# Fused attention, Fourier mixing and two feed-forward stages: tables split on the host, g_norm moved to the head outputs, the start reordered

## The chip, the cores and the metric

The kernel runs on one core of a Trainium2 chip. The metric is device microseconds of one execution. Three runs of the kernel before took 1918.46 to 1920.63 us, median 1919.91.

## The reference

Three layers, all in float32, with batch 8, 8 heads, sequence 576, head size 64, model width 512:

```python
kv  = einsum('bhsd,bhse->bhde', k, v)
out = einsum('bhsd,bhde->bhse', q, kv)
x   = out / sqrt(mean(out*out, -1) + 1e-06) * g_norm     # per head, then heads side by side
u   = x + real(fft(fft(x, axis=1), axis=2))              # sequence, then width
un  = (u - mean(u)) / sqrt(var(u) + 1e-06)
x2  = u + relu(un @ w_ch1) @ w_ch2                       # 512 -> 2048 -> 512
u2  = x2 + (x2.T @ U @ V).T                              # rank 32 over the sequence
y   = u2 + relu(u2 @ w1b) @ w2b
```

The weights of both feed-forward stages arrive as 64-bit floats (seen by the kernel as pairs of 32-bit words) and are made 32-bit on the chip.

## The kernel before

**Precision by splitting.** Most matmuls use operands of type fp32r, a rounded float32. A number is held as a high part (a copy on ACT, which rounds) and a low part (the number less the high part, on DVE or POOL). A product is three matmuls: low by high, high by low, high by high. Names end in `h` and `l`.

**The main loop** has 18 blocks of 512 tokens, 9 for the first feed-forward stage (phase A) and 9 for the second (phase B), with 16 steps each. Step `n` loads one 128-wide strip of the hidden layer: `split_w2` and `split_w1` (two steps ahead) split the weights, `emit_l1` runs 12 matmuls into `h`, ACT makes `gh` (line 174) and DVE `gl` (line 175), and `emit_l2` of the step before runs 12 matmuls that need `gl`. Then the step's side tasks follow. On each engine instructions run in the order in which this code issues them; a step's `gl` on DVE therefore stands behind all that the side tasks of the step before put on DVE.

**Side tasks.** While block `j` of phase A runs, `batch_tasks(j + 1)` prepares the next batch: `t_o` (q times kv into PSUM; ACT squares it, line 265, and copies it out, line 266; DVE sums the squares, line 268; POOL raises to the power -1/2, line 270), `t_norm` (DVE multiplies by that, line 281; POOL multiplies by `g_norm`, line 283), `t_fold_s`/`t_fold_e` (sums and differences of mirrored tokens and columns, lines 296, 297 and 302), `t_fold_h`/`t_fold_l` (their high and low parts; `pile` for the last tokens), `t_s1` (Fourier along the sequence), `t_s2` (along the width, and the update of `x`). In block 0 the side tasks also hold 13 steps of `w_conv`, the conversion of a pair of weight tiles: a load into one of two `raw` buffers, two ACT and three DVE instructions per tile, and a POOL addition (line 98). The load of the next pair waits for the conversion of this one.

**The start** does batch 0 in line, before the loop: kv, q, the five tiles of `t_o`, `t_norm` (all of it on DVE and ACT here), folds, `t_s1`, `t_s2`, then the row statistics (`t_ln`: `bn_stats`, line 472), four transposes (`t_tr`) and the first `emit_l1`. `load_tables` fetches six tables of cosines and sines, `split_table` splits them on ACT and POOL. Three weight pairs are converted in between. All loads and stores are issued by SP, in order.

Of the kernel before, what the change touches and what calls it, by code (L numbers as in the profile page):

```python
# [34 lines left out]

HMIN, HMAX = (float(v) for v in np.array([0x38000000, 0x47EFFFFF], np.uint32).view(np.float32))
# [3 lines left out]
def kernel(ctx: ExitStack, tc: tile.TileContext, qT, kvm, gn, w1a, w2a, w1b, w2b,  # L40
# [5 lines left out]
    wpool = ctx.enter_context(tc.tile_pool(name="wpool", bufs=NF))  # L46
# [5 lines left out]
    ps_s = ctx.enter_context(tc.tile_pool(name="ps_s", bufs=2, space=PSUM))  # L52

# [21 lines left out]
    def raw_load(src, n):  # L75

        r = com.tile([128, 512, 2], U32, tag="raw", name="raw", bufs=2)
        nc.sync.dma_start(out=r[:, 0:n].rearrange("p n w -> p (n w)"), in_=src.bitcast(U32))
        return r[:, 0:n]

    def conv_a(raw, out):
# [5 lines left out]
        pw = com.tile([128, 512], U32, tag="cv1", name="cv1", bufs=2)[:, 0:n]  # L87
# [110 lines left out]
    pa = ctx.enter_context(tc.tile_pool(name="pa", bufs=1))  # L198
# [40 lines left out]
    def t_kv(b, half):  # L239
# [10 lines left out]
        nc.vector.tensor_copy(out=kvbd[64:128, pairs, 64:128], in_=pv[64:128, :, 64:128])  # L250
# [3 lines left out]
    def t_o(b, k):  # L254
# [11 lines left out]
        nc.scalar.activation(out=s["x"][:m, g, c, :], in_=ps[:m, :], func=AF.Copy)  # L266
# [5 lines left out]
    def t_norm(b, k):  # L272
# [4 lines left out]
        if b == 0 and g == 1:  # L277
# [4 lines left out]
        eng = nc.vector if b == 0 else nc.gpsimd  # L282
        eng.tensor_tensor(out=xv, in0=xv, in1=gnb[:m].unsqueeze(1).to_broadcast([m, H, D]), op=ALU.mult)
# [3 lines left out]
    def t_fold_s(b, c):  # L287
        s = st[b]
        if c == 0:
# [6 lines left out]
        nc.vector.tensor_tensor(out=f[:m, 0, c, 0:DM], in0=x[:m, 0, c], in1=x[:m, 1, c], op=ALU.add)  # L296
        nc.gpsimd.tensor_tensor(out=f[:m, 1, c, 0:DM], in0=x[:m, 0, c], in1=x[:m, 1, c], op=ALU.subtract)
# [110 lines left out]
    def batch_tasks(b):  # L408
# [3 lines left out]
        for c in range(3):  # L412
# [3 lines left out]
            t[c + d + 3] += [lambda c=c: t_fold_s(b, c), lambda c=c: t_fold_e(b, c, 0), lambda c=c: t_fold_h(b, c, 0)]  # L416
# [30 lines left out]

    def t_ln_load(j):
        un[j] = [pa.tile([128, DM], F32, tag="un", name=f"un{j}_{t}", bufs=4) for t in range(4)]
        for t in range(4):  # L450
            load_u(un[j][t], 4 * j + t)

    def t_ln_first(cc):

        x = st[0]["x"]
        if cc == 0:
            un[0] = [pa.tile([128, DM], F32, tag="un", name=f"un0_{t}", bufs=4) for t in range(4)]
# [9 lines left out]
    def t_ln(j, ts=range(4)):  # L467
        if 0 in ts:
            lns[j] = [pa.tile([128, 4, w], F32, tag=f"ln{w}", name=f"ln{j}_{w}") for w in (6, 2, 1)]
# [69 lines left out]
    def x_new(j):  # L539
        pool = pa if j % 2 else pbx["pb"]  # L540
        return tuple(pool.tile([128, 4, BT], F32R, tag=t, name=f"{t}b{j}") for t in ("xh", "xl"))

    def t_b_tables(step):
# [68 lines left out]
    def t_u2(j, dc):  # L612
        pb = pbx["pb"]
        blk = NB + j
        if dc == 0 and j:
# [53 lines left out]
    CONV = (1, 1, 0, 1, 13)  # L669
# [10 lines left out]
    with tc.manual_schedule():  # L680
# [7 lines left out]
        nc.sync.dma_start(out=gnb, in_=gn)  # L688
        w_load(0)
        w_load(1)  # L690
        load_tables()
# [202 lines left out]
```

## Time and profile before

| | |
|---|---|
| profiled execution | 1920.98 us, span 1919.2 us |
| median of three runs | 1919.91 us |
| busy | PE 1816.7, DVE 966.8, ACT 773.9, POOL 751.5 us |
| start, until the first `h` matmul | 75.25 us |
| block 0, until the first `h` matmul of step 16 | 150.05 us |
| blocks 1 to 6 | 111.9 or 113.4 us each |

PE is the matmul engine (PEld its weight loads), DVE the vector engine, ACT the scalar engine, POOL GpSimd, SP the queue of transfers. Times are microseconds from the span's start. PEclk is the granted clock of the matmul engine as a share of full speed. A wait is put down to what came last.

### The profile page before, as it was taken

Reading aid. Unit: us, or ns where it says so; the run is one execution under the profiler, and the core shown is the slowest. Engines: PE = TensorE matmul, PEld = TensorE weight load, DVE = VectorE, ACT = ScalarE, POOL = GpSimd, SP = SyncE. Lnnn points to the kernel's source line nnn. Section 1 sums busy time; section 2 is a strip of 40 time slices with the busy share of each in tenths; the row PEclk is TensorE's granted clock in tenths of the full one; section 3 lists DMA queues with packets and bytes.
Section 4 is the critical chain, followed back from the end, with each engine's and each line's share of the span. In section 5 each row is a group of like instructions: output and inputs, shape, how many; then the busy total and the mean of one; then the engine's idle time right before and its main releaser. Section 6 shows DMA issues by size and latency. Waiting matters only on the chain.

```text
span 1919.2 us, 22748 instructions
## 1 busy us (share of the span) xinstructions
PE 1816.7 (95%) x8520; PEld 1504.9 (78%) x8520; DVE 966.8 (50%) x1458; ACT 773.9 (40%) x1462; POOL 751.5 (39%) x592
## 2 busy tenths in 40 slices
PE   3767999999999999999999999999999999999999
PEld 3646878788787878878888888888888888888887
DVE  5887875757757575755443333333333233333222
ACT  4445543444444344433434343334333343333332
POOL 4576554555445555533322223222222222222322
PEclk7889999999999999999999999999999999999999
DMA  4524424142242414202223201010101010100000
GB/s 148 208 101 168 170 90 146 56 165 106 109 135 86 158 56 160 89 12 81 72 99 109 84 0 50 1 44 1 50 1 44 1 50 1 45 1 22 1 23 23
DMA packets 61760, 142.14 MB, mean 74 GB/s; under 512 B 11129, under 2 KB 13898, under 8 KB 58834
## 3 DMA queue, kind: packets, MB, share of 16 engines
q1 hardware_dynamic: 61650, 140.69, 20.9%
q8 instruction: 67, 1.10, 0.2%
q14 instruction: 43, 0.35, 0.1%
HBM read 102.88 MB, written 36.73 MB: 73 GB/s over the span
## 4 chain that ended last, share of the span: by engine, by line
PE 81%; DVE 9%; POOL 4%; ACT 3%; issue 2%; DMA 1%; SPq 0%; DVEq 0%; POOLq 0%; ACTq 0%
PE h L169 12%; PE h L171 12%; PE h L170 12%; PE acc L195 7%; PE acc L194 7%; PE acc L193 7%; PE acc L189 5%; PE acc L191 5%; PE acc L190 5%; DVE f L302 2%; PE kv L245 2%; DVE eh L331 1%; POOL ss L270 1%; PE o L263 1%; PE pt L603 1%
## 5 line engine op out<-in xcount | busy, mean ns | idle before, releaser
L147 POOL TENSOR_TENSOR w1l<-w,w1h 128x512 fp32r<-128x512 f32 x274 | 355.5, 1297 | 971.7 <-ACT w1h L146 948.4
L175 DVE SCALAR_TENSOR_TENSOR gl<-h,gh 128x512 fp32r<-128x512 f32 x288 | 198.3, 689 | 389.7 <-ACT gh L174 389.5
L174 ACT ACTIVATE gh<-h 128x512 fp32r<-128x512 f32 x288 | 171.5, 596 | 500.5 <-PE h L171 500.4
L155 DVE TENSOR_TENSOR w2l<-w,w2h 128x512 fp32r<-128x512 f32 x283 | 231.8, 819 | 188.6 <-ACT w2h L154 187.8
L189 PE MATMUL acc<-w2h,gl 128*128 128x512 f32 x576 | 233.8, 406 | 41.2 <-DVE gl L175 41.1
L154 ACT ACTIVATE w2h<-w 128x512 fp32r<-128x512 f32 x288 | 181.2, 629 | 159.5 <-PE acc L195 112.0
L190 PE MATMUL acc<-w2l,gh 128*128 128x512 f32 x576 | 230.0, 399 | 10.0 <-POOL w2l L155 10.0
L169 PE MATMUL h<-xl,w1h 128*128 128x512 f32 x576 | 228.6, 397 | 1.4 <-DVE xl L493 1.4
L169 PE MATMUL h<-xlb,w1h 128*128 128x512 f32 x576 | 229.8, 399 | 0.0
L191 PE MATMUL acc<-w2h,gh 128*128 128x512 f32 x576 | 229.4, 398 | 0.0
L171 PE MATMUL h<-xhb,w1l 128*128 128x512 f32 x576 | 226.8, 394 | 0.0
L170 PE MATMUL h<-xhb,w1h 128*128 128x512 f32 x576 | 226.6, 393 | 0.0
L171 PE MATMUL h<-xh,w1l 128*128 128x512 f32 x576 | 225.4, 391 | 0.8 <-POOL w1l L147 0.8
L195 PE MATMUL acc<-gh,w2h 128*128 128x512 f32 x576 | 225.0, 391 | 0.0
L170 PE MATMUL h<-xh,w1h 128*128 128x512 f32 x576 | 224.8, 390 | 0.0
L194 PE MATMUL acc<-gl,w2h 128*128 128x512 f32 x576 | 224.7, 390 | 0.0
L193 PE MATMUL acc<-gh,w2l 128*128 128x512 f32 x576 | 224.4, 390 | 0.0
L146 ACT ACTIVATE w1h<-w 128x512 fp32r<-128x512 f32 x288 | 179.9, 625 | 35.5 <-POOL w L98 35.5
L189 PEld LDWEIGHTS acc<-w2h,gl 128*128 128x128 f32 x576 | 111.1, 193 | 74.5 <-DVE gl L175 51.4
L190 PEld LDWEIGHTS acc<-w2l,gh 128*128 128x128 f32 x576 | 111.5, 194 | 33.5 <-POOL w2l L155 11.4
L191 PEld LDWEIGHTS acc<-w2h,gh 128*128 128x128 f32 x576 | 111.2, 193 | 24.0
L169 PEld LDWEIGHTS h<-xlb,w1h 128*128 128x128 f32 x576 | 108.3, 188 | 25.5 <-issue 2.6
(162 smaller groups left out, 2731.8 us busy)
## 6 DMA issues: line engine op xcount, KB each, us to landing
kv<-in_kvm SPq DMA_DIRECT2D x14, 1280.0 KB, 8.3
q<-in_qT SPq DMA_DIRECT2D x8, 1220.0 KB, 7.5
x_d<-x2o SPq DMA_DIRECT2D x36, 256.0 KB, 2.1
x2f<-x_d SPq DMA_DIRECT2D x36, 256.0 KB, 4.0
outT<-o SPq DMA_DIRECT2D x36, 256.0 KB, 2.0
raw<-in_w1a SPq DMA_DIRECT2D x16, 512.0 KB, 10.1
raw<-in_w2a SPq DMA_DIRECT2D x16, 512.0 KB, 4.2
u_d<-x SPq DMA_DIRECT2D x32, 256.0 KB, 2.5
```

The costliest lines, as they stand in the source:

```text
L147: (nc.vector if n in on_dve else nc.gpsimd).tensor_tensor(out=al, in0=a, in1=f32(ah), op=ALU.subtract)
L155: (nc.gpsimd if n in CLP else nc.vector).tensor_tensor(out=cl, in0=c, in1=f32(ch), op=ALU.subtract)
L169: nc.tensor.matmul(out=h, lhsT=ah[:, kc, :], rhs=xl[:, kc, :], start=(kc == 0), stop=False)
L170: nc.tensor.matmul(out=h, lhsT=ah[:, kc, :], rhs=xh[:, kc, :], start=False, stop=False)
L171: nc.tensor.matmul(out=h, lhsT=al[:, kc, :], rhs=xh[:, kc, :], start=False, stop=(kc == 3))
L175: nc.vector.scalar_tensor_tensor(out=gl, in0=h, scalar=0.0, in1=f32(gh), op0=ALU.max, op1=ALU.subtract)
L189: nc.tensor.matmul(out=a, lhsT=gl[:, tt], rhs=ch, start=s, stop=False)
L190: nc.tensor.matmul(out=a, lhsT=gh[:, tt], rhs=cl, start=False, stop=False)
L191: nc.tensor.matmul(out=a, lhsT=gh[:, tt], rhs=ch, start=False, stop=e)
L193: nc.tensor.matmul(out=a, lhsT=cl[:, tt], rhs=gh, start=s, stop=False)
L194: nc.tensor.matmul(out=a, lhsT=ch[:, tt], rhs=gl, start=False, stop=False)
L195: nc.tensor.matmul(out=a, lhsT=ch[:, tt], rhs=gh, start=False, stop=e)
```

## The change

- The tables are split on the host. They arrive as three tensors, are copied by DMA to a DRAM tile and from there to SBUF; `split_table` is gone.
- `t_o`: DVE multiplies the PSUM tile by `g_norm` into `x`, in place of ACT's copy. `t_norm` has no second multiplication left. The squares are still taken of the unscaled tile.
- `t_norm` of batch 1 has the tiles of `g == 1` on ACT (eight scalings each), as batch 0 has. Both `kvbd` copies of batch 1 are on ACT.
- The difference folds of batch 0 are on DVE, with those of later batches still on POOL.
- In the start: the second Fourier stage takes slices 2, 0, 1; the first weight conversions come after `t_s1` and between the slices; row statistics are taken in two parts; the second weight pair is converted after `t_ln`, and `split_w1(0)` comes earlier.
- `un` and `res` are single tiles of four; in phase B the even blocks use their buffers; pools are opened in another order.

```diff
-    def load_tables(): ...
-    def split_table(nm): ...
+    def load_tables(step, t={}):
+        for k, src in enumerate(tabs):
+            if step == 0:
+                t[k] = dram.tile(list(src.shape), F32, tag=f"tab_d{k}", name=f"tab_d{k}")
+                nc.sync.dma_start(out=t[k], in_=src)
+                continue
+            s = at.tile(list(src.shape), F32R, name=f"tab{k}")
+            nc.sync.dma_start(out=f32(s), in_=t[k])
...
 def t_kv
-        nc.vector.tensor_copy(out=kvbd[64:128, pairs, 64:128], in_=pv[64:128, :, 64:128])
+        if b == 1:
+            nc.scalar.activation(out=kvbd[64:128, pairs, 64:128], in_=pv[64:128, :, 64:128], func=AF.Copy)
+        else:
+            nc.vector.tensor_copy(out=kvbd[64:128, pairs, 64:128], in_=pv[64:128, :, 64:128])
...
 def t_o
-        nc.scalar.activation(out=s["x"][:m, g, c, :], in_=ps[:m, :], func=AF.Copy)
+        nc.vector.tensor_tensor(out=heads(s["x"][:m, g, c]), in0=heads(ps[:m, :]),
+                                in1=gnb[:m].unsqueeze(1).to_broadcast([m, H, D]), op=ALU.mult)
...
 def t_norm
-        if b == 0 and g == 1:
+        if b < 2 and g == 1:
...
-        eng = nc.vector if b == 0 else nc.gpsimd
-        eng.tensor_tensor(out=xv, in0=xv, in1=gnb[:m].unsqueeze(1).to_broadcast([m, H, D]), op=ALU.mult)
...
 def t_fold_s
+        eng = nc.gpsimd if b and p else nc.vector
+        eng.tensor_tensor(out=f[:m, p, c, 0:DM], in0=x[:m, 0, c], in1=x[:m, 1, c], op=(ALU.add, ALU.subtract)[p])
...
 def x_new
-        pool = pa if j % 2 else pbx["pb"]
+        tags = ("xh", "xl") if j % 2 else ("un", "res")
+        pools = (pa, pa if j else pbx["pb"])
...
 the start
+        load_tables(0)
         w_load(0)
         w_load(1)
-        load_tables()
+        load_tables(1)
...
+        for p in range(2):
+            for e in range(2):
+                t_s1(0, p, e)
+        conv_b(*conv_a(raws.pop(0), w_new(0)))
+        t_s2(0, 2)
+        t_ln_first(2)
         t_s2(0, 0)
         t_ln_first(0)
+        split_w1(0)
+        t_s2(0, 1)
+        t_ln_first(1)
+        t_ln_stats(0, (0, 2))
+        conv_b(*conv_a(raws.pop(1), w_new(1)))
         w_next((0, 1))
+        t_ln_stats(0, (1, 3))
         load_q(1)
-        conv(CONV[1])
-        split_w1(0)
         t_kv(1, 0)
         t_kv(1, 1)
...
         t_ln(0)
-        conv(CONV[2])
+        conv(1)
         for t in range(4):
             t_tr(0, t)
```

Three places show what moves. The first is DVE in the start, from the end of `t_o` to the first folds of batch 0 (`x` is the batch's tile, `f` the folded one); before:

```order
L268 TENSOR_REDUCE ss_199<-sq_198 98x8 [waits Activation_49]
L269 TENSOR_SCALAR ss_199<-ss_199 98x8 [waits DVE_49]
L281 TENSOR_TENSOR x_197<-x_197,ss_199 128x512 [waits Pool_49]
L283 TENSOR_TENSOR x_197<-x_197,gnb 128x512 [waits DMAHW5_49,DVE_49]
L283 TENSOR_TENSOR x_197<-x_197,gnb 128x512 [waits Activation_49]
L296 TENSOR_TENSOR f_261<-x_197 128x512 [waits DMAHW2_49,DMAHW1_49,DMAHW3_49,DMAHW0_49,DVE_49]
L302 TENSOR_TENSOR f_261<-f_261 128x256 [waits DVE_49]
```

And in the change:

```order
L266 TENSOR_TENSOR x_208<-o_4_251,gnb 98x512 [waits Activation_49]
L269 TENSOR_REDUCE ss_210<-sq_209 98x8
L270 TENSOR_SCALAR ss_210<-ss_210 98x8 [waits DVE_49]
L282 TENSOR_TENSOR x_208<-x_208,ss_210 128x512 [waits Pool_49]
L296 TENSOR_TENSOR f_270<-x_208 128x512 [waits DMAHW1_49,DMAHW2_49,DMAHW0_49,DMAHW3_49,DVE_49]
L301 TENSOR_TENSOR f_270<-f_270 128x256 [waits DVE_49]
```

The multiplication by `gnb` has moved ahead of the sums, one for each of five tiles, and now it is the one that waits for ACT's square; the two behind the scaling are gone.

The second is DVE between the second Fourier stage and the first transposes (`cv` and `w` are weight conversions, `ln` the row statistics); before:

```order
L385 TENSOR_TENSOR x_197<-x_197,de_2_469 34x255 [waits DVE_49]
L89 TENSOR_SCALAR cv_482<-cv_482 128x512 [waits Activation_49]
L91 TENSOR_SCALAR w_0_1_480<-cv_482 128x512 [waits DVE_49]
L89 TENSOR_SCALAR cv_487<-cv_487 128x512 [waits Activation_49]
L91 TENSOR_SCALAR w_0_1_481<-cv_487 128x512 [waits DVE_49]
L96 SCALAR_TENSOR_TENSOR cv_482<-raw 128x512 [waits DMAHW3_49]
L96 SCALAR_TENSOR_TENSOR cv_487<-raw 128x512 [waits DMAHW4_49,DVE_49,Activation_49]
L250 COPY kvbd<-kv_0_504 64x2x64 [waits Activation_49]
L250 COPY kvbd<-kv_1_517 64x2x64 [waits Activation_49]
L472 BN_STATS ln_6_536<-un_0_418 128x6 [waits DMAHW0_49]
```

And in the change, from the last row statistics on:

```order
L476 BN_STATS ln_6_448<-un_393 128x6 [waits DMAHW5_49,DMAHW3_49]
L477 BN_AGGR ln_2_449<-ln_6_448 128x2 [waits DVE_49]
L481 TENSOR_SCALAR ln_1_450<-ln_2_449 128x4 [waits DVE_49]
L484 TENSOR_SCALAR un_393<-un_393,ln_2_449,ln_1_450 128x512 [waits Pool_49]
L484 TENSOR_SCALAR un_393<-un_393,ln_2_449,ln_1_450 128x512 x3
L96 TENSOR_SCALAR cv_513<-cv_513 128x512 [waits Activation_49]
L98 TENSOR_SCALAR w_0_1_511<-cv_513 128x512 [waits DVE_49]
L96 TENSOR_SCALAR cv_518<-cv_518 128x512 [waits Activation_49]
L98 TENSOR_SCALAR w_0_1_512<-cv_518 128x512 [waits DVE_49]
L103 SCALAR_TENSOR_TENSOR cv_513<-raw 128x512 [waits DMAHW6_49]
L103 SCALAR_TENSOR_TENSOR cv_518<-raw 128x512 [waits DMAHW7_49,DVE_49,Activation_49]
L499 TENSOR_TENSOR xl_532<-tr_0_533,xh_531 128x4x128 [waits Activation_49]
```

The conversion of the second weight pair stood ahead of the statistics and stands behind them now, still ahead of what the first matmuls wait for; the copies of `kvbd` have left DVE.

The third is POOL in steps 17 to 20 of the loop, that is in block 1 (`ss` is the power -1/2, `f` the difference fold, `w1l` the weights' low part); before:

```order
L283 TENSOR_TENSOR x_1810<-x_1810,gnb 128x512 x2
L270 TENSOR_TENSOR ss_1812<-ss_1812,nhalf 128x8 x2
L283 TENSOR_TENSOR x_1810<-x_1810,gnb 128x512 x2
L270 TENSOR_TENSOR ss_1812<-ss_1812,nhalf 98x8
L147 TENSOR_TENSOR w1l_1993<-w_0_5_797,w1h_1992 128x512
L297 TENSOR_TENSOR f_2008<-x_1810 128x512
L283 TENSOR_TENSOR x_1810<-x_1810,gnb 98x512
```

And in the change:

```order
L271 TENSOR_TENSOR ss_1793<-ss_1793,nhalf 128x8 x2
L271 TENSOR_TENSOR ss_1793<-ss_1793,nhalf 98x8
L154 TENSOR_TENSOR w1l_1970<-w_0_5_780,w1h_1969 128x512
L296 TENSOR_TENSOR f_1985<-x_1791 128x512
L154 TENSOR_TENSOR w1l_2017<-w_0_6_856,w1h_2016 128x512
```

Five multiplications are gone from POOL; what is left of the batch there stands in the same order.

## Rows read from the trace of the kernel before

**Rows 1.** Windows, four stretches: stretch and length, busy us by engine, PEclk, DMA
```profile
0.00:75.25 75.25, 32.72 (x203) 30.88 (x203) 49.17 (x86) 31.25 (x77) 34.13 (x33) 0.77 0.56 193
75.25:225.30 150.05, 121.08 (x547) 97.45 (x548) 123.02 (x176) 74.55 (x143) 101.81 (x74) 0.91 0.41 146
225.30:905.70 680.40, 653.94 (x3281) 550.02 (x3280) 451.74 (x691) 291.32 (x589) 344.30 (x274) 0.99 0.30 104
905.70:1919.20 1013.50, 1008.97 (x4494) 826.50 (x4492) 342.89 (x506) 376.81 (x654) 271.27 (x212) 1.00 0.10 34
```
**Rows 2.** PE's waits from 75 to 200 us: us in total, times, longest
```profile
PE acc L189 <- DVE gl L175: 14.0, 7, 4.6
PE acc L190 <- POOL w2l L155: 10.0, 4, 2.8
```
**Rows 3.** PE's waits from 200 to 900 us, the only row
```profile
PE acc L189 <- DVE gl L175: 27.1, 19, 2.3
```
**Rows 4.** Timeline of the start: start, us, instruction, [idle before it <- releaser]
```profile
16.69 0.69 DVE L268 TENSOR_REDUCE ss<-sq 128x8 f32<-128x512 f32 x1 [1.43 <-ACT sq L265]
...
17.67 8.27 POOL L270 TENSOR_TENSOR ss<-ss,nhalf 128x8 f32<-128x8 f32 x5 [16.36 <-DVE ss L269]
...
20.97 2.02 ACT L279 ACTIVATE x<-x,ss 128x64 f32<-128x64 f32 x8
...
27.75 2.98 DVE L283 TENSOR_TENSOR x<-x,gnb 128x512 f32<-128x512 f32 x2
...
31.49 1.37 DVE L302 TENSOR_TENSOR f<-f 128x256 f32<-128x256 f32 x1
...
40.07 0.58 PE L342 MATMUL s<-csh,eh 128*128 128x290 f32 x1 [20.49 <-ACT ez L307]
...
44.07 0.30 PE L342 MATMUL s<-ssh,eh 128*128 128x290 f32 x1
```
**Rows 5.** Windows, the loads of the start (columns as in rows 1)
```profile
10.00:20.00 10.00, 9.34 (x69) 8.93 (x68) 3.53 (x9) 4.48 (x11) 2.33 (x2) 1.00 0.93 342
```
**Rows 6.** DVE's timeline, the last update of x in the start
```profile
56.75 0.94 DVE L385 TENSOR_TENSOR x<-x,de 34x255 f32<-34x255 f32 x1
```
**Rows 7.** Chain of waits that ended last, in the start: start, us, what
```profile
54.21 7.26 DMA raw<-in_w2a
...
64.90 0.70 DVE ln L472
...
70.16 3.69 PE tr L488 x16
...
75.25 0.50 PE h L169
```
**Rows 8.** POOL's timeline in block 0
```profile
98.57 2.53 POOL L283 TENSOR_TENSOR x<-x,gnb 128x512 f32<-128x512 f32 x2 [1.64 <-ACT cv L88]
...
120.88 1.27 POOL L283 TENSOR_TENSOR x<-x,gnb 98x512 f32<-98x512 f32 x1 [0.63 <-DVE x L281]
```
**Rows 9.** DVE's timeline in block 0
```profile
105.06 3.25 DVE L281 TENSOR_TENSOR x<-x,ss 128x512 f32<-128x512 f32 x2
```
**Rows 10.** Windows, blocks 1 and 2; blocks 3 and 5 read as 1, 4 as 2
```profile
229.70:341.60 111.90, 107.47 (x550) 90.61 (x548) 76.28 (x117) 48.56 (x100) 58.05 (x47) 1.00 0.34 116
341.60:455.10 113.50, 109.10 (x550) 91.83 (x548) 76.28 (x117) 48.66 (x100) 58.03 (x47) 0.98 0.32 115
```
**Rows 11.** DVE's timeline in block 1
```profile
229.42 1.28 DVE L505 TENSOR_TENSOR x2o<-acc,res 128x512 f32<-128x512 f32 x2
...
252.71 1.77 DVE L281 TENSOR_TENSOR x<-x,ss 98x512 f32<-98x512 f32 x1
...
262.22 0.42 DVE L302 TENSOR_TENSOR f<-f 128x256 f32<-128x256 f32 x1
```
**Rows 12.** ACT's timeline in block 1
```profile
255.88 0.63 ACT L285 ACTIVATE x<-x 34x512 f32<-34x512 f32 x1 [2.50 <-POOL x L283]
```
**Rows 13.** Line 175 from 200 to 900 us: ns at least, median, at most
```profile
L175 DVE SCALAR_TENSOR_TENSOR gl<-h,gh x100: 677/684/692, 201.5 to 890.1; 128x512 fp32r<-128x512 f32 x100
```

More of the change, by code (lines that the diff above doesn't have):

```diff
@@ L75, in raw_load @@
     def raw_load(src, n):
-        r = com.tile([128, 512, 2], U32, tag="raw", name="raw", bufs=2)
+        r = cvp.tile([128, 512, 2], U32, tag="raw", name="raw", bufs=2)
         nc.sync.dma_start(out=r[:, 0:n].rearrange("p n w -> p (n w)"), in_=src.bitcast(U32))
@@ L195, in emit_l2 @@
                 nc.tensor.matmul(out=a, lhsT=ch[:, tt], rhs=gh, start=False, stop=e)
-    pa = ctx.enter_context(tc.tile_pool(name="pa", bufs=1))
+    for t in ("xh", "xl", "un", "res"):
+        pa.tile([128, 4, BT], F32, tag=t, name="first_" + t)
     att_ctx = ExitStack()
@@ L446, with un_new @@
     lns = {}
+    def un_new(j):
+        u = pa.tile([128, 4, DM], F32, tag="un", name=f"un{j}")
+        un[j] = [u[:, t] for t in range(4)]
     def t_ln_load(j):
-        un[j] = [pa.tile([128, DM], F32, tag="un", name=f"un{j}_{t}", bufs=4) for t in range(4)]
+        un_new(j)
         for t in range(4):
@@ L455, in t_ln_first @@
         x = st[0]["x"]
-        if cc == 0:
-            un[0] = [pa.tile([128, DM], F32, tag="un", name=f"un0_{t}", bufs=4) for t in range(4)]
+        if 0 not in un:
+            un_new(0)
         pos = 0
@@ L465, in t_ln_first, with t_ln_stats @@
             pos += m
-    def t_ln(j, ts=range(4)):
-        if 0 in ts:
+    def t_ln_stats(j, ts):
+        if j not in lns:
             lns[j] = [pa.tile([128, 4, w], F32, tag=f"ln{w}", name=f"ln{j}_{w}") for w in (6, 2, 1)]
@@ L614, in t_u2 @@
         blk = NB + j
-        if dc == 0 and j:
+        if dc == 0:
             xt[blk] = x_new(j)
@@ L749 @@
         split_w1(1)
-        conv(CONV[3])
+        conv(1)
         early.clear()
@@ L823, in _tables @@
     sd = np.where(k % 256 == 0, 0.0, np.sin(2 * np.pi * k / DM)) * live
-    last = lambda a, n: np.concatenate([a[256:288], a[256:288], a[256:n]])
-    out = {"cz": last(cs, 289), "sz": last(ss, 288)}
-    for nm, a in (("cs", cs), ("ss", ss), ("cd", cd), ("sd", sd)):
-        out[nm] = a[:256].reshape(2, 128, -1).transpose(1, 0, 2).reshape(128, -1)
-    return {nm: np.ascontiguousarray(a.astype(np.float32)) for nm, a in out.items()}
+    out = {}
+    for nm, a, n in (("cs", cs, 289), ("ss", ss, 288), ("cd", cd, 0), ("sd", sd, 0)):
+        hi, lo = _split(a)
+        for v, w in ((hi, "h"), (lo, "l")):
+            out[nm + w] = v[:256].reshape(2, 128, -1).transpose(1, 0, 2).reshape(128, -1)
+        if n:
+            out[nm[0] + "z"] = np.concatenate([hi[256:288], lo[256:288], hi[256:n]])
+            if n == 289:
+                z = out["z288"] = np.zeros((97, a.shape[1]), np.float32)
+                z[32] = hi[288]
+    full = []
+    for names in TABS:
+        full.append(np.zeros((128, sum(n for _, _, n in names)), np.float32))
+        o = 0
+        for nm, p, n in names:
+            full[-1][:p, o:o + n] = out[nm]
+            o += n
+    return full
 def kernel(**inputs):
@@ L884 @@
     out = nc.dram_tensor("outT", (DM, NT), F32, kind="ExternalOutput").ap()
-    tabs = {n: aps.pop(n) for n in _tables()}
+    tabs = [aps.pop(f"tab{k}") for k in range(len(TABS))]
     with tile.TileContext(nc) as tc:
```

114 lines of the change are left out of this document (46 added, 68 removed).

## The prediction

> **What bounds the kernel now.** I read the busy time by stretch first [rows 1]. Phase B, the last 1013.50 us, has TensorE busy for 1008.97 at the full clock (1.00, the 2.4 GHz level): nothing is to be had there except fewer matmuls, and the change takes none away. The reader is to see that the idle time lies in front. The start lasts 75.25 us with PE busy for 32.72. Block 0 lasts 150.05 us with PE busy for 121.08, DVE for 123.02 and POOL for 101.81. Blocks 1 to 6 together last 680.40 us with PE busy for 653.94, so 26.46 are idle.
>
> Then the waits by what ended them: in block 0 PE waits 14.0 us for `gl` and 10.0 for POOL's `w2l` [rows 2]; in blocks 1 to 6 the only row is 27.1 us for `gl` in 19 waits, the longest 2.3 [rows 3], that is about three waits and 4.5 us in a block. One block alone agrees: 111.90 long with PE busy 107.47, so 4.43 idle [rows 10]. Last the timelines and the chain that ended last: in the start it runs through the first scaling and folds [rows 4], the last update of `x` [rows 6], the load of a raw weight, the statistics and the transposes [rows 7].
>
> Two prices come from DVE's rows. An SBUF operation of DVE beside a busy POOL is stretched: line 281 takes 1.77 and, in block 0, 3.25 for two [rows 9, 11]; the fold of line 302 takes 1.37 in the start and 0.42 where POOL does nothing [rows 4, 11]. An operation with a PSUM input isn't: line 175 stays between 677 and 692 ns over 100 times [rows 13]. So POOL's 283 lengthens exactly what stands around it. The new multiplication has a PSUM input. Its nearest row is line 505, PSUM by SBUF of the same shape, two in 1.28, that is 0.68 for one and 0.60 from start to start [rows 11]. I price it at 0.60 in a run of operations.
>
> **The change, part by part.** The sum is made against the profiled execution, 1920.98 us (span 1919.2 and 1.78 around it), 1.07 above the median of the runs.
>
> *Start, first stage.* DVE now does for each of five tiles a multiplication (0.60), a sum (0.69, [rows 4]) and the small operation behind it (0.13, from its share of the 0.98 between the sum's start and the first power): 1.42, so from 16.69 to 23.8. The powers take 8.27/5 = 1.65 each [rows 4], so the sums keep ahead of them; the last ends near 26.5, 0.6 later than now. DVE scales the first tile (0.69) by 24.5; ACT's eight scalings of the second (2.02) are done by 23.6. A sum fold costs 0.69 + 0.42 = 1.1 without POOL beside it, so the first ends at 25.6. ACT takes its high part (0.5) and the next eight scalings to 28.2, the second fold ends at 29.3, the last tile's scaling at 30.0, ACT's copy (0.63, [rows 12]) at 30.7, the third fold at 31.8, its high and low part near 32.5. The first cosine matmul starts there and not at 40.07 [rows 4]: −7.6. What goes are five multiplications behind the scaling (2.98 for two, [rows 4]), the tables' splits on ACT and POOL, and so the stretch (1.37 against 0.42). Against it the difference folds come to DVE: after the cosine half's lows (about 34.2) three times 1.1 and two lows of 0.42 give 38.3 for the sine half, which starts at 44.07 now: −5.8. The sine half is the later one, so −5.8 goes on to the last update of `x`, which ends at 56.75 + 0.94 = 57.69 now [rows 6] and at 51.9 then.
>
> *Tables through DRAM.* By the shapes, 2.69 MB go into the DRAM tile, then two raw weights (1.05 MB), then 2.69 MB into SBUF. The start's loads move 342 GB/s with a busy share of 0.93 [rows 5]. At that rate, from about 13.4, the copy ends at 21.3, the weights at 24.4, the cosine table at 27 and the last at 32.3: ahead of 32.5. No row shows a copy from DRAM to DRAM. Were it at half the rate, the cosine table would land at 34 to 35, which the sine half's 38.3 hides but for 1.5 at most; at the full rate it costs nothing. I take nothing, and keep 1.5.
>
> *Start, second part.* Now a raw weight's load ends at 54.21 + 7.26 = 61.47, its conversion stands on DVE ahead of the statistics, and these start at 64.90 [rows 7]. Then they no longer wait for it. What stays is the transfer of `x` to `un`, which no row prices alone: at most the 7.2 us from 57.69 to 64.90, at least about 2; I take 3, since it moves less than the 7.26 load and meets no other load. Statistics then start at 54.9. From there to the first `h` matmul it takes 75.25 − 64.90 = 10.35 now; 0.6 less as half of the statistics are done ahead, so 64.6. The moved conversion's six DVE operations (near 2.9 us) lie beside the transposes, 3.69 on PE. Start: −10.5, between −6 (the transfer takes 7.2 and the tables cost 1.5, less what the statistics give) and −13.
>
> *Block 0.* Two pairs and one single multiplication leave POOL, 2.53 for the first pair and 1.27 for the single one [rows 8], together 6.3, and POOL's own waits for PE are 10.0 [rows 2]. DVE gets 5 × 0.60 = 3.0 more and loses two scalings of about 1.6 [rows 9], which go to ACT (2 × 2.02, less five copies near 0.5). A walk through the steps brings the `gl` of the batch's busiest step about 4 earlier. The 13 conversions stay, with their load of the next pair behind the conversion of this one, and carry the shift along without enlarging it. Block 0: −4. Its lower end, −9, is POOL's 6.3 and the stretch of two scalings (1.4 each); its upper, +4, is the 4.0 added to ACT with nothing back.
>
> *Blocks 1 to 6.* The three waits of a block lie where the batch is normalised: line 281 (1.77), POOL's 283 (1.27), then ACT's copy, which was idle for 2.50 until POOL had done [rows 12], and behind it on ACT the step's `w2h` and `gh`, and so `gl`. Without 283 the copy follows the scaling: −1.3 for POOL, −1.2 for the scaling (1.77 to 0.6), −1.0 for each fold (1.37 to 0.42), −0.6 as the powers on POOL no longer queue behind multiplications. Against it 5 × 0.60 = 3.0 of DVE, spread over three steps. The latest `gl` comes about 4.1 earlier, and of 4.5 idle 3.7 go: 6 × 3.7 = −22, between 0 and −4.5 a block. Blocks 2, 4, 6 are 113.50 at a clock of 0.98, their neighbours 111.90 at 1.00 [rows 10], with the same matmuls. I take two of the three dips, 1.5 each, as gone where the idle time before them goes: −3.
>
> *Phase B* has other buffers and the same work: 0, within its idle 4.5 either way.
>
> Sum: 1920.98 − 10.5 − 4 − 22 − 3 = 1881.5, and 1.07 less on the median's scale, rounded to **1881**.
>
> The Trainium skill, in "VectorE: DVE Perf Modes", section "The DRAIN you can't avoid", has the next DVE operation start only when the pipe of the one before is empty; the page's formula for a tensor by tensor operation of 512 floats, (512 + 151)/0.96, gives 691 ns. By that each new multiplication costs 0.69 and not 0.60, 0.45 more for five and 2.7 more over six blocks: 1884 as an estimate. The pair in 1.28 [rows 11] is shorter than twice 0.69, so the row is taken.
>
> **The rivals.** (a) *The five multiplications eat what the contention gives back.* DVE's 3.0 a block stands in the same steps as the waits, and the sums wait behind them. For it: DVE is where the waits end [rows 3]. Against: ACT's idle 2.50 and the stretch are larger together. Blocks 1 to 6 unchanged: 1920.98 − 10.5 − 4 = 1906.
> (b) *Slower: the multiplication at PSUM lengthens the wait for `gl`.* If POOL's multiplication isn't what stretches line 281 and the copy on ACT wasn't on the path, each block pays 3.0 (18 in all), block 0 pays 5 (DVE's 3.0 and ACT's 4.0 less 2.4), and the start gives only 6: 1920.98 − 6 + 5 + 18 = 1938. With the start and block 0 so, it decides from 0.8 us a block on (−1 + 6 × 0.8 = 3.8). Against it: 1.77 beside POOL, 0.42 for a fold without [rows 11].
> (c) *More goes.* All of 27.1 and the three dips (4.5), block 0 by 9, the start by 13: 1867.
> That the tables come too late is the way in which the change would not do what it says; it would need a third of the 342 GB/s for all 6.43 MB to cost over 25 us, and I count it with (b).
>
> **How the numbers follow.** The forecast has 0.70, (a) 0.15, (c) 0.09, (b) with late tables 0.06. About 0.2%, 3.8 us, is what a measurement of this kernel can tell from no change. Faster 0.93 (a tail of (a), 0.01, falls within), same 0.02, slower 0.05. The forecast's own range, 1872 to 1893, is the start's −6 to −13 and 3.0 to 4.4 a block. The range takes in (a) and most of (c): 1864 to 1908.
>
> **What would show it.** In the profile after: the first `h` matmul at 64 to 65, the first cosine matmul at 32.5 and the first sine matmul at 38.3, neither waiting for a transfer; block 0 about 146 long; blocks 1 to 6 107 to 109 each, with waits on `gl` of 1 us or less a block and no second kind of length; POOL without some 35 multiplications, DVE's folds near 0.42. It is wrong if the first Fourier matmuls wait for the tables, if `gl` waits stay at 4 a block, or if PE waits for something new in block 0.

## The result, and the profile after

The changed kernel takes 1893.32 us (median of four runs, 1892.45 to 1895.47) against 1920.13: ratio 0.9862, 95% interval 0.985 to 0.9874. It is 26.8 us faster, the interval clear of 1; 1881 was forecast, so 12 of the 39 us are missing. The profiled execution took 1892.45, its span 1890.6.

Here and below block 0 is taken to the second step of block 1 (one step further than in [rows 1], where PE's work on the next batch begins), so that all kernels are cut alike. The last stretch begins with step 2 of block 7: the prediction called it phase B, but two blocks of phase A without a batch are in it. Windows of the kernel before with that border (block 0, blocks 1 to 6; stretch and length, busy us of PE, PEld, DVE, ACT and POOL, PEclk, DMA):

```profile
75.20:229.70 154.50, 125.48 (x575) 101.37 (x575) 124.48 (x178) 76.11 (x147) 102.18 (x75) 0.91 0.41 145
229.70:905.70 676.00, 649.54 (x3255) 546.10 (x3254) 450.27 (x689) 289.80 (x587) 343.97 (x274) 0.99 0.30 104
```

And of the changed kernel, all four stretches:

```profile
0.00:65.00 65.00, 33.17 (x202) 30.84 (x202) 39.35 (x87) 26.58 (x65) 22.16 (x24) 0.80 0.75 267
65.00:222.10 157.10, 128.76 (x573) 104.38 (x574) 121.57 (x181) 78.07 (x157) 95.87 (x70) 0.89 0.42 151
222.10:883.80 661.70, 647.47 (x3255) 545.90 (x3254) 451.93 (x719) 276.26 (x557) 303.92 (x244) 0.99 0.30 107
883.80:1890.60 1006.80, 1002.95 (x4494) 826.69 (x4492) 343.06 (x506) 376.81 (x654) 271.82 (x212) 1.00 0.10 34
```

Set side by side, in us, the four stretches came out differently:

| | before | after | difference | forecast |
|---|---|---|---|---|
| start | 75.2 | 65.0 | −10.2 | −10.5 |
| block 0 | 154.5 | 157.1 | +2.6 | −4 |
| blocks 1 to 6 | 676.0 | 661.7 | −14.3 | −25 with the clock |
| last stretch | 1013.5 | 1006.8 | −6.7 | 0 |

**The start** came out at the size worked out. DVE's and PE's timelines (start, us, instruction, [idle before <- releaser]):

```profile
16.00 0.69 DVE L266 TENSOR_TENSOR x<-o,gnb 128x512 f32<-128x512 f32 x1 [1.43 <-ACT sq L264]
16.61 0.68 DVE L269 TENSOR_REDUCE ss<-sq 128x8 f32<-128x512 f32 x1
...
24.47 0.42 DVE L301 TENSOR_TENSOR f<-f 128x256 f32<-128x256 f32 x1
...
62.49 2.48 DVE L499 TENSOR_TENSOR xl<-tr,xh 128x512 fp32r<-128x512 f32 x4
```

```profile
31.46 0.58 PE L341 MATMUL s<-tab,eh 128*128 128x290 f32 x1 [12.57 <-DVE eh L330]
...
36.95 0.37 PE L341 MATMUL s<-tab,eh 128*128 128x290 f32 x1 [0.96 <-PE s L347]
...
65.02 0.79 PE L176 MATMUL h<-xl,w1h 128*128 128x512 f32 x1 [3.82 <-DVE xl L499]
```

The new multiplication is followed 0.61 later by the sum; the fold takes 0.42 where [rows 4] had 1.37; the cosine half starts at 31.46 (32.5 forecast), waiting for DVE and not for a table, the sine half at 36.95 (38.3), the first `h` at 65.02 (64.6). The end of the start, from the chain that ended last and from DVE's timeline:

```profile
47.67 4.66 DMA un<-x
```

```profile
55.63 0.67 DVE L476 BATCH_NORM_STATS2 ln<-un 128x6 f32<-128x512 f32 x1
```

The slice of `x` on that chain is done at 47.7 and its transfer to `un` lands 4.7 later. The very last update of `x`, on POOL, ends at 50.2.

**Block 0.** Its steps 0 and 1, whose `h` matmuls follow each other in one run, last 17.0 us together and 10.8 before; the rest 140.1 and 143.7. (The expectations call the two "step 0" and count the steps behind them one lower than the loop does; the text here counts as the loop.) The two steps before, then in the changed kernel:

```profile
75.20:86.00 10.80, 10.16 (x51) 8.41 (x52) 8.45 (x14) 7.27 (x13) 6.00 (x5) 1.00 0.29 99
```

```profile
65.00:82.00 17.00, 14.17 (x53) 11.33 (x53) 9.55 (x15) 7.86 (x14) 7.67 (x6) 0.76 0.45 149
```

Of the 6.2 us, 4.0 are matmuls that take longer (PE busy 14.17 and not 10.16, at a mean granted clock of 0.76 and not 1.00) and 2.2 are waiting. Until 69.5 the `h` matmuls start 0.43 us apart, at the 1.2 GHz level, and from there 0.23 apart; behind the wait for `gl` they are 0.43 apart again, from 77.0 to 80.0. From 55 to 65 PE had been busy for 2.7 of 10 us. In the kernel before, the low level was over when the first `h` began: there they start 0.23 apart from the second on.

The waiting comes from SP's queue. SP's queue before, then SP's queue and its wait, and ACT, DVE and PE, of the changed kernel:

```profile
63.81 0.33 SPq L78 DMA_DIRECT2D raw<-in_w1a  x1
...
64.75 0.43 SPq L392 DMA_DIRECT2D u_d<-x  x1
```

```profile
57.43 0.48 SPq L393 DMA_DIRECT2D u_d<-x  x1
64.42 0.32 SPq L391 DMA_DIRECT2D u_d<-x  x1
...
65.22 0.36 SPq L85 DMA_DIRECT2D raw<-in_w1a  x1
```

```profile
SPq L391 <- DMA u_d<-x: 6.4, 1, 6.4
```

```profile
69.41 0.68 ACT L95 ACTIVATE cv<-raw 128x512 f32<-128x512 f32 x1 [5.05 <-DMA raw<-in_w1a]
...
72.31 0.58 ACT L181 ACTIVATE gh<-h 128x512 fp32r<-128x512 f32 x1
...
75.04 0.68 DVE L182 SCALAR_TENSOR_TENSOR gl<-h,gh 128x512 fp32r<-128x512 f32 x1
...
75.87 0.47 PE L196 MATMUL acc<-w2h,gl 128*128 128x512 f32 x1 [2.81 <-DVE gl L182]
```

SP stands 6.5 us at the fifth store of `u` (57.9 to 64.4, until an earlier store has landed; by lines 390 to 393 the fifth writes row 288, which the second has written), and the third weight pair is queued behind it. It lands at 69.4. Four operations of ACT on it stand ahead of `gh`, and six of DVE and `w2l` ahead of `gl`, which so comes at 75.0. In the kernel before SP stands at the fifth store too, but the pair is issued ahead of the stores, and 11 us ahead of the first `h`.

**Blocks 1 to 6.** PE's waits from 220 to 885 us (us in total, times, longest), and ACT and DVE in block 2:

```profile
PE acc L196 <- DVE gl L182: 14.2, 12, 2.2
```

```profile
355.45 1.78 DVE L282 TENSOR_TENSOR x<-x,ss 98x512 f32<-98x512 f32 x1
...
357.26 0.63 ACT L284 ACTIVATE x<-x 34x512 f32<-34x512 f32 x1 [1.13 <-DVE x L282]
...
370.66 0.42 ACT L306 ACTIVATE ez<-f 32x256 fp32r<-32x256 f32 x1 [2.40 <-DVE f L301]
...
372.37 0.20 ACT L324 ACTIVATE xe<-f 33x1 f32<-33x1 f32 x1
372.48 0.61 ACT L161 ACTIVATE w2h<-w 128x512 fp32r<-128x512 f32 x1
373.00 0.58 ACT L181 ACTIVATE gh<-h 128x512 fp32r<-128x512 f32 x1
```

Of 27.1 us [rows 3], 14.2 are left. The waits of steps 5 and 6 (1.4 and 0.8 a block) fell to nothing and 0.2; that of step 7, 2.2, is what it was. ACT's copy waits 1.13 for the scaling where it waited 2.50 for POOL [rows 12], but the scaling itself still takes 1.78 [rows 11]: POOL's `w1l` and difference fold stand beside it now as before. The wait of 2.2 has another owner: five small operations of ACT on the last tokens' fold, which wait for DVE (lines 306 to 308, 321 and 324, from 370.66 to 372.57), stand ahead of `w2h` and `gh`.

### The profile page after: what moved, and what is told of

Its sections match the earlier page's. It is cut to its first block, busy times and chain, and to the rows that moved or that the text cites. A ratio compares the mean times of both kernels' runs of the same rounds, so it can differ in the third digit from the quotient of the medians.

```text
span 1890.6 us, 22610 instructions
## 1 busy us (share of the span) xinstructions
PE 1812.4 (96%) x8520; PEld 1507.8 (80%) x8520; DVE 955.9 (51%) x1492; ACT 757.7 (40%) x1432; POOL 693.8 (37%) x548
## 4 chain that ended last, share of the span: by engine, by line
PE 81%; DVE 12%; ACT 3%; DMA 2%; issue 1%; POOL 0%; SPq 0%; DVEq 0%; ACTq 0%; POOLq 0%
PE h L176 12%; PE h L178 12%; PE h L177 12%; PE acc L202 7%; PE acc L201 7%; PE acc L200 7%; PE acc L196 5%; PE acc L198 5%; PE acc L197 5%; DVE f L301 2%; PE kv L241 2%; DVE eh L330 1%; DVE w2l L162 1%; PE o L262 1%; DMA raw<-in_w1a 1%; DVE gl L182 1%
## 5 line engine op out<-in xcount | busy, mean ns | idle before, releaser
L197 PE MATMUL acc<-w2l,gh 128*128 128x512 f32 x576 | 230.4, 400 | 10.2 <-POOL w2l L162 10.2
L198 PEld LDWEIGHTS acc<-w2h,gh 128*128 128x128 f32 x576 | 111.3, 193 | 23.7
L176 PEld LDWEIGHTS h<-xl,w1h 128*128 128x128 f32 x576 | 109.6, 190 | 25.6 <-DVE xl L499 4.2
```

What stands on the lines that cost most here:

```text
L176: nc.tensor.matmul(out=h, lhsT=ah[:, kc, :], rhs=xl[:, kc, :], start=(kc == 0), stop=False)
L197: nc.tensor.matmul(out=a, lhsT=gh[:, tt], rhs=cl, start=False, stop=False)
L198: nc.tensor.matmul(out=a, lhsT=gh[:, tt], rhs=ch, start=False, stop=e)
```

## The experiments

Stage lengths are from each kernel's own profile, cut as above. One profile is one execution: in the changed kernel, e3 to e6 and e11, whose code for the start is the same, the first `h` comes between 64.6 and 67.1, so a difference of a microsecond or two in the start or in the first two steps may be chance.

**Stores behind the conversion (e1).**

```diff
-        for c in range(3):
-            t_u_out(0, c)
         t_ln(0)
         conv(1)
         ...
         conv(1)
+        for c in range(3):
+            t_u_out(0, c)
```

> The changed kernel with the six stores of batch 0's u moved behind the second weight conversion of the start on SP. Theory: step 0 of block 0 lasts 17.0 us (10.8 before) because SP stands at the fifth store from 57.9 to 64.4 and the next weight pair is issued only at 65.2; with the stores behind it the pair is issued at about 62.6 as line 103 ends, lands 2.6 earlier, and step 0 shrinks to about 14.4; time 1890.7 against 1893.3. Rival: the pair's place on ACT ahead of the first gh is what counts and the stores only compete for bandwidth: step 0 stays at 16.5 to 17, time within 1 us of 1893.3.

Measured 1890.76 (ratio to the kernel before 0.9847, 0.9831 to 0.9864). SP, and the windows (steps 0 and 1, the rest of block 0):

```profile
62.34 0.33 SPq L85 DMA_DIRECT2D raw<-in_w1a  x1
...
70.48 0.42 SPq L391 DMA_DIRECT2D u_d<-x  x1
```

```profile
65.30:77.70 12.40, 12.38 (x52) 10.32 (x53) 7.21 (x13) 7.28 (x13) 5.78 (x4) 0.79 0.62 205
77.70:220.00 142.30, 114.18 (x525) 92.16 (x523) 114.41 (x169) 70.66 (x145) 90.16 (x66) 0.92 0.42 151
```

The pair is issued at 62.3 and the first two steps last 12.4 and not 17.0 (14.4 expected); the steps behind it take 2.2 of the 4.6 back (142.3 against 140.1). The theory stands: the wait of 2.8 is gone, and with it 1.8 of PE's own time (12.38 and not 14.17), as the granted clock no longer falls behind that wait. That the two steps still last 12.4 and not 10.8, with PE busy throughout, is the clock: 0.79 of full, the mean of stretches at 1.2 and at 2.4 GHz, behind a start in which PE was idle half of the time.

**The conversion behind the first `gh` (e2).**

```diff
         split_w1(1)
-        conv(1)
...
             emit_l1(n)
+            if n == 0:
+                conv(1)
```

> The changed kernel with the conversion of the third weight pair of the start moved behind the first gh and gl (in step 0, ahead of the split of step 2's weights). Theory: gh of step 0 waits on ACT behind four operations on weights that land at 69.4 only; without them it runs at 70.2 and not 72.3, the first acc matmul starts at 73 and not 75.9, and step 0 loses about 3 us; time 1890.3. Rival: the late weights are waited for anyway, now by the h matmuls of step 2, and the sum of steps 0 to 2 (30.7 us) stays: 1893.3.

Measured 1894.47 (0.9868, 0.9853 to 0.9882). Windows of steps 0 and 1, and of step 2:

```profile
65.90:78.50 12.60, 12.58 (x53) 10.40 (x53) 5.26 (x8) 3.48 (x6) 4.33 (x4) 0.78 0.47 152
78.50:91.20 12.70, 9.27 (x43) 7.22 (x42) 11.12 (x21) 8.55 (x15) 7.53 (x5) 0.87 0.29 110
```

The rival won: steps 0 and 1 got 4.4 shorter, step 2 5.4 longer (12.7 against 7.3). Letting others pass the late weights only moves the wait; bringing the weights earlier (e1) takes it away.

**High parts of the last tokens one step later (e3).**

```diff
-            t[c + d + 3] += [lambda c=c: t_fold_e(b, c, 0), lambda c=c: t_fold_h(b, c, 0)]
+            t[c + d + 3] += [lambda c=c: t_fold_e(b, c, 0)]
+            t[c + d + (4 if c == 2 else 3)].append(lambda c=c: t_fold_h(b, c, 0))
```

> The changed kernel with the high parts of the last tokens' sum fold (five operations of ACT) moved one step later, behind the next gh. Theory: what is left of the waits in blocks 1 to 6, 2.2 us a block, comes from these five, which stand on ACT ahead of w2h and gh and wait for DVE's fold, and has nothing to do with the multiplication by g_norm; moved, the wait goes: blocks 1 to 6 together 661.7 - 13 = 649, time 1880. Rival: the wait is only handed to the next step, whose gh now stands behind them: blocks unchanged at 661.7, time 1893.

Measured 1877.44 (0.9775, 0.9759 to 0.9791). Its waits in blocks 1 to 6, and the window of these blocks:

```profile
PE acc L196 <- DVE gl L182: 4.8, 12, 0.6
```

```profile
222.50:871.40 648.90, 644.11 (x3255) 543.18 (x3254) 451.43 (x719) 276.08 (x557) 304.87 (x244) 1.00 0.31 109
```

12.8 us shorter, as expected: the five operations owned the wait. The long and the short blocks are gone: blocks 1 to 5 last 108.1 each (109.7 or 111.3 in the changed kernel). The edit moves the fold of batch 1 too, and block 0 is 1.7 shorter (155.4), which with the scatter of the runs (1876.4 to 1880.1) may be why the time is below the 1880 expected.

**g_norm back on POOL for batches 2 to 7 (e4).**

```diff
-        nc.vector.tensor_tensor(out=heads(s["x"][:m, g, c]), ...
+        if b < 2: ...                       # as in the change
+        else:
+            nc.scalar.activation(out=s["x"][:m, g, c, :], in_=ps[:m, :], func=AF.Copy)
...
+        if b >= 2:
+            nc.gpsimd.tensor_tensor(out=xv, in0=xv, in1=gnb[:m]..., op=ALU.mult)
```

> The changed kernel with g_norm for batches 2 to 7 again on POOL in t_norm, and ACT's copy in t_o (blocks 1 to 6 only). Theory: the move of g_norm alone is what took 2.0 us a block: waits for gl come back to 4.4 us a block, blocks 1 to 6 from 661.7 to about 674 to 676, time 1906 to 1908; start, block 0 and phase B as in the changed kernel. Rival: the gain of blocks 1 to 6 came from something else of the change (buffers, the order of the pools): blocks within 3 us of 661.7.

Measured 1908.79 (0.9941, 0.9924 to 0.9958; 1906 to 1908 expected). Its waits and the window of blocks 1 to 6:

```profile
PE acc L196 <- DVE gl L182: 26.7, 18, 2.2
```

```profile
223.00:897.30 674.30, 647.58 (x3255) 543.87 (x3254) 450.41 (x689) 289.59 (x587) 344.43 (x274) 1.00 0.30 105
```

26.7 is the 27.1 of [rows 3] again, in 18 waits. The place of `g_norm` made the waits of steps 5 and 6, and only these. The edit brings back two things at once, the multiplication on POOL and the copy on ACT; no run parts them.

**Buffers of phase B as before (e5).**

```diff
-        tags = ("xh", "xl") if j % 2 else ("un", "res")
-        pools = (pa, pa if j else pbx["pb"])
-        return tuple(p.tile([128, 4, BT], F32R, tag=t, ...) for p, t, nm in ...)
+        pool = pa if j % 2 else pbx["pb"]
+        return tuple(pool.tile([128, 4, BT], F32R, tag=t, ...) for t in ("xh", "xl"))
```

> The changed kernel with the buffers of x in phase B as before: the odd blocks in the pool of phase A, the even ones in phase B's own pool. Theory: the 6.7 us that phase B got shorter come from where x lies in SBUF: the h matmuls of blocks 10 to 17 start 231 ns apart in the kernel before and 228 in the changed one; with the old buffers phase B is 1012 to 1014 us again, time 1899 to 1900. Rival: other tiles (weights, tables) that moved with the pools set the pitch: phase B stays at 1007, time 1893.

Measured 1898.31 (0.988, 0.9863 to 0.9896). The last stretch:

```profile
884.50:1897.30 1012.80, 1008.96 (x4494) 826.59 (x4492) 342.86 (x506) 376.86 (x654) 272.15 (x212) 1.00 0.10 34
```

The same 4494 matmuls take 6.0 longer. By blocks it is sharper than expected: the `h` matmuls start 233.5 to 233.8 ns apart in blocks 9, 11, 13, 15 and 17, whose `x` lies in phase B's own pool, and 227.2 to 228.4 in the blocks between; the kernel before has the same numbers, and the changed kernel 226.6 to 228.5 in all blocks of phase B but block 9 (232.5), whose low part is still in that pool.

The traces say that a matmul isn't slow by the place of its own moving operand alone. In block 9 of the changed kernel the matmuls that read the high part, which lies in the fast place, are as slow as those that read the low part (start to start 232.3 and 233.5 against 232.0 ns). And in blocks 11, 13 and 15 of e5 the first three `acc` matmuls of a step are 231 to 233 ns apart (226 to 227 in the blocks between), though none of their operands has moved.

**The same, shifted by 32 bytes (e11).**

```diff
             pb = pbx["pb"] = ctx.enter_context(tc.tile_pool(name="pb", bufs=1))
+            nc.vector.memset(pb.tile([128, 8], F32, name="pad"), 0.0)
```

> The kernel of e5 (phase B's buffers of x as before) with a tile of 32 bytes a partition, written once and never read, allocated first in phase B's own pool, so that x of blocks 9, 11, 13, 15 and 17 lies 32 bytes further on in SBUF. In e5 the h matmuls of these five blocks start 233.6 ns apart and those of the blocks between 227 to 228, whose x lies in phase A's pool at addresses 32 off a multiple of 64; in phase B's pool it lies at a multiple of 64. Theory: the alignment sets the pitch: 228 in all blocks, the last stretch 1006 to 1007, time 1892. Rival: the region does (phase B's pool lies above 190 KB of the partition, phase A's x below 45 KB): still 233.6, 1012.8, time 1898.

Measured 1899.51 (0.9896, 0.988 to 0.9913). The last stretch:

```profile
885.60:1897.60 1012.00, 1008.12 (x4495) 825.72 (x4492) 343.04 (x507) 377.07 (x654) 272.01 (x212) 1.00 0.11 34
```

The five blocks stay at 233.2 to 233.4 ns. So these 32 bytes are not what differs, and the region is what is left of the two: by the addresses of the programs, the matmuls are slow with `x` at 143424 (before) and 191296 bytes (e5) of the partition and fast at 106400 (before), 28576 and 44960 (changed). Where between 122784 (the end of the fast low part) and 143424 a border lies, whether a larger offset or what else lies there matters, and by what mechanism, these runs don't tell.

**The second pair's conversion ahead of the statistics (e7).**

```diff
-        t_ln(0)
         conv(1)
+        t_ln(0)
```

> The changed kernel with the conversion of the second weight pair of the start ahead of the last part of the row statistics again, as before the change. Theory: the statistics then wait for the pair, which lands at about 59, and the first h matmul moves from 65.0 to 68.5 to 69.5; but the third pair's load waits for the same conversion as now, so step 0 loses what the start adds: end of step 0 within 1.5 us of 82, time 1892 to 1895. Rival: the whole delay is kept, as step 0 waits for other things: time 1897.

Measured 1894.18 (0.9859, 0.9845 to 0.9874). Start, and steps 0 and 1:

```profile
0.00:71.50 71.50, 32.79 (x203) 30.65 (x203) 40.83 (x87) 27.05 (x66) 22.22 (x24) 0.74 0.72 260
71.50:83.30 11.80, 11.80 (x53) 9.92 (x53) 9.28 (x15) 7.09 (x13) 6.56 (x5) 0.84 0.25 90
```

The first `h` comes 6.5 later, more than the 3.5 to 4.5 expected, but step 1 ends at 83.3 against 82.0, and the time is the changed kernel's within a microsecond, which four runs each can't tell from nothing. In these two steps PE is busy throughout (11.80 of 11.80): of the 5.2 us that they are shorter than in the changed kernel, 2.8 are waiting and 2.4 the clock (0.84 and not 0.76). This step of the reordering moved 6.5 us out of the start, and 5.2 of them came back in the first two steps.

**Difference folds of batch 0 on POOL (e8).**

```diff
-        eng = nc.gpsimd if b and p else nc.vector
+        eng = nc.gpsimd if p else nc.vector
```

> The changed kernel with the difference folds of batch 0 on POOL, as before the change. Theory: POOL's three folds run beside DVE's sum folds and stretch them, so the cosine half starts 1 to 2 us after 31.5, while DVE saves three folds of 0.69 behind it and the sine half stays at 36 to 37: time within 1.5 us of 1893.3. Rival: POOL's folds are plain help, cosine at 31.5 and sine at 35, time 1891; or the stretch is paid in both halves, sine at 39, time 1895.5.

Measured 1894.85 (0.9863, 0.9848 to 0.9878). DVE's fold, and PE's first cosine matmul:

```profile
28.98 1.37 DVE L301 TENSOR_TENSOR f<-f 128x256 f32<-128x256 f32 x1
```

```profile
34.17 0.58 PE L341 MATMUL s<-tab,eh 128*128 128x290 f32 x1 [15.39 <-DVE eh L330]
```

The fold is back at 1.37 (0.42 in the changed kernel) and the cosine half starts 2.7 later, more than expected. The sine half doesn't stay, as the theory had it: it starts at 38.57, 1.6 later, and the first `h` comes at 66.6. Whether the stretch beside POOL costs more than POOL's help is worth isn't shown: kernels with the changed kernel's start have a first `h` as late as 67.1, and the two medians, 1.5 apart, are of runs that overlap (1893.1 to 1896.2 against 1892.5 to 1895.5).

**g_norm alone, on the kernel before (e10).**

```diff
-        nc.scalar.activation(out=s["x"][:m, g, c, :], in_=ps[:m, :], func=AF.Copy)
+        nc.vector.tensor_tensor(out=heads(s["x"][:m, g, c]), in0=heads(ps[:m, :]),
+                                in1=gnb[:m].unsqueeze(1).to_broadcast([m, H, D]), op=ALU.mult)
...
-        eng = nc.vector if b == 0 else nc.gpsimd
-        eng.tensor_tensor(out=xv, in0=xv, in1=gnb[:m]..., op=ALU.mult)
```

> The kernel before with one part of the change alone: g_norm applied by DVE in t_o, for all batches, and no second multiplication in t_norm. Theory: blocks 1 to 6 lose the waits of steps 4 and 5, 2.0 us a block (676 to about 662 with one clock dip less), block 0 loses about 3 in its steps 3 to 5 and gains no long step 0, the start loses about 4 (five multiplications of 1.5 against five of 0.6 in PSUM's order), phase B stays at 1013.5: time 1920 - 14 - 3 - 4 = 1899. Rival: the start's gain needs the rest of the change (tables, order), and block 0 is bound by its conversions: 1920 - 13 = 1907.

Measured 1898.16 (0.9885, 0.9868 to 0.9901). Start, block 0 and blocks 1 to 6 (the last stretch has 1013.2):

```profile
0.00:70.60 70.60, 31.60 (x202) 29.75 (x202) 47.43 (x86) 29.44 (x72) 34.61 (x33) 0.78 0.59 206
70.60:224.40 153.80, 127.76 (x574) 103.40 (x575) 124.95 (x183) 74.40 (x141) 95.84 (x70) 0.90 0.40 146
224.40:883.10 658.70, 644.70 (x3256) 544.39 (x3254) 451.67 (x719) 276.55 (x557) 303.48 (x244) 1.00 0.30 107
```

This one part gives 22 of the 27 us: 4.6 in the start, 0.7 in block 0 (3 expected), 17.3 in blocks 1 to 6. All the rest of the change adds −5.6 in the start, +3.3 in block 0, −6.4 in the last stretch, and +3 in blocks 1 to 6, half of it one more clock dip (a few us in which the granted clock falls to the 1.2 GHz level). So what the split tables and the new order of the start were made for comes to 2.3 us, start and block 0 together; no run parts the tables from the order.

**Scalings of batch 1 back on DVE (e6).**

```diff
-        if b < 2 and g == 1:
+        if b == 0 and g == 1:
```

> The changed kernel with the two scalings of batch 1 that went to ACT back on DVE (block 0 only). Theory of the prediction: they relieve DVE by 1.6 each and put 2.0 each on ACT, a small gain in steps 3 to 5; without them block 0 is 1 to 2 us longer than 157.1: time 1894 to 1895. Rival: ACT's eight scalings stand ahead of gh and cost more than they save; block 0 gets 1 to 3 shorter: time 1891.

Measured 1894.41 (0.9868, 0.9853 to 0.9883). Block 0:

```profile
66.40:226.30 159.90, 130.40 (x574) 105.14 (x575) 123.75 (x183) 74.76 (x141) 95.87 (x70) 0.88 0.41 148
```

2.8 longer than in the changed kernel. But 1.0 of it lies in the first two steps, ahead of any scaling; the steps behind take 141.9, and 140.0 to 140.5 in the changed kernel, e4, e5, e8 and e11, which change nothing there. So 1.4 to 1.9 are the scalings' in this profile, as the theory had it, and the profile is of the slowest of four runs. The medians are 1.1 apart, too little to be told from nothing.

**Both edits (e9),** e1 and e3 together.

> The changed kernel with two edits: the six stores of u behind the second conversion (e1) and the high parts of the last tokens one step later (e3). Theory: they act in different stretches (step 0 of block 0; blocks 1 to 6), so they add: 1893.3 - 2.5 - 15.9 = 1875. Rival: block 0 absorbs the earlier start of step 0 in its later waits: 1877.4, as with the second alone.

Measured 1875.76 (0.9765, 0.975 to 0.9779), four runs from 1875.28 to 1876.65: faster than either kernel. They add nearly as expected, 17.6 of 18.4. Block 0 and blocks 1 to 6:

```profile
66.40:217.50 151.10, 125.26 (x573) 101.71 (x574) 120.29 (x181) 78.08 (x157) 95.87 (x70) 0.91 0.44 159
217.50:866.40 648.90, 644.30 (x3256) 543.28 (x3255) 451.30 (x719) 276.14 (x557) 305.03 (x244) 1.00 0.30 109
```

## Why the prediction was right and where it was wrong

*Faster, mainly by the move of `g_norm`: right* (e4, e10). The measured 1893 lies in the range, 12 above the forecast. In part that is luck: 6.7 of the 26.8 us come from phase B, which was forecast at nothing, and without them the time would have been 1900, nearer to rival (a)'s 1906 than to 1881. (The forecast's own range, 1872 to 1893, comes out of its parts only if the clock's 3 is taken as 4.5 at the lower end and as nothing at the upper, and the upper leaves out the 1.07.)

*Start, −10.5: right in size, −10.2, and by its own steps up to the sine half; behind it two errors cancel.* Multiplications at 0.60, folds at 0.42, tables not on the path, the second weight pair behind the statistics: each shows in the trace. Then the update of `x` on the chain ends at 47.7 where 51.9 was forecast, 4.2 early, and the last statistics begin 8.0 behind it where 3 were forecast: the transfer takes 4.7, and one tile's conversion of the first weight pair still stands on DVE between the two halves of the statistics (53.2 to 54.9). The Trainium skill's rule weighed there ("VectorE: DVE Perf Modes", section "The DRAIN you can't avoid") isn't what the row shows: the sum starts 0.61 after the multiplication, which itself lasts 0.69, so the row's 0.60 was the better price. The same section of the Trainium skill adds that a next operation that isn't held starts earlier, and with that the trace agrees.

*Block 0, −4: wrong, by the sentence that the conversions "carry the shift along without enlarging it".* The steps behind the first two gave 3.6, about what was forecast for them. The first two took 6.2 more, and the prediction's own sign of being wrong, a new wait of PE in block 0, is there: 2.8 us for `gl`. The sum had no term for SP's queue, where the reordering put the stores of `u` ahead of the third weight pair, and none for the clock of these steps. A stage that starts 10 us earlier needs its weights 10 us earlier, and it began while the granted clock was still at the 1.2 GHz level: e1 shows the queue's part to be 2.6 in time by the medians, and leaves 1.6 of the 6.2, with no wait, to the clock; e7 shows 6.5 us of the start's gain to come back as 5.2 of loss in the first two steps.

*Blocks 1 to 6, −3.7 each: mechanism right, size wrong; the term that failed is step 7's wait, "of 4.5 idle 3.7 go".* Steps 5 and 6 went as worked out, 2.0 us. The wait of 2.2 was taken to lie where the batch is normalised, like them, since it stood in the same row [rows 3] with the same releaser; e3 shows another chain behind the same name. Of the four prices in the sum, POOL's 1.3 and the powers' queueing are seen; the stretch of line 281 and of the folds (1.2 and 1.0) stayed, because POOL's `w1l` and fold stand there too.

*The clock, −3: right in mechanism, and tied to the wrong wait.* In the changed kernel two of six blocks are still 1.5 longer (three before). Windows of step 7 of block 1 and of block 2:

```profile
258.10:269.70 11.60, 9.45 (x41) 7.69 (x41) 6.59 (x12) 6.68 (x15) 2.57 (x2) 0.85 0.26 83
369.30:379.40 10.10, 7.95 (x42) 6.61 (x41) 6.69 (x12) 6.59 (x15) 1.90 (x2) 1.00 0.12 22
```

Both have the wait of 2.2; in one of them the granted clock falls to a mean of 0.85 behind it (part of the step at the 1.2 GHz level), in the other not. Where e3 and e9 leave 0.6 of that wait, none of their twelve blocks has the longer step 7. So the wait cost 2.2 and now and then 1.5 more. How often varies from run to run: with this wait left as it is, one block has it in e4 and in e10, two in the changed kernel and three in e1, so the one dip less is not shown to be the change's.

*Phase B, 0: wrong, −6.7.* I had costed new buffers at nothing because no instruction changed, and had taken it that only fewer matmuls could shorten the stretch. e5 gives 6.0 to the place of `x`, and e11 that an offset of 32 bytes doesn't matter; the mechanism stays open.

The rivals: (a), blocks 1 to 6 unchanged, is refuted by the 14.3 us and by e4. (b) found a right place for a loss, block 0, but not its mechanism. (c) would have needed the wait that the change doesn't touch; e9, which takes it away, comes to 1876.

## What to carry to other kernels

A row of waits with one releaser can hold several chains: follow one wait of each length back through its engine's queue before counting them all as one term. When a stage is made to start earlier, list every transfer that must arrive earlier too, and what stands ahead of it in its queue, and look at the granted clock of the stretch into which its matmuls move, or the gain comes back one step on. With POOL's multiplication gone and its `w1l` and fold left, DVE's line 282 still took 1.78: before pricing a stretch beside POOL as gone, list all of POOL's operations there.

## What the runs showed of the hardware that I had not expected

The place of `x` in SBUF changes the pitch of matmuls: 6.0 us over 1012.8 with the same instructions at the same clock (e5), and not by an offset of 32 bytes (e11). It slows matmuls beside those that read the moved tile, too: with the low part alone in the slow place all `h` matmuls of block 9 are at 232 to 234 ns, and in e5 the first `acc` matmuls behind the `h` are slower as well. A wait of 2.2 us before the same matmuls is followed by a lower granted clock in one to three of six blocks, a wait of 0.6 in none of twelve.
